# A gated scan and top-1 experts on one core: one page for the expert with most tokens left in place of the last pair of pages, sums of squares of late weights on ScalarE, a load stock of 6500

## The chip, the core and the metric

The kernel runs on one core of one Trainium2 chip. The core has five engines that run side by side and wait for each other by semaphores: TensorE (PE, matmuls; its weight loads are listed apart as PEld), VectorE (DVE), ScalarE (ACT), GpSimd (POOL) and SyncE (SP, which here only issues transfers). Transfers run on 16 DMA engines. The metric is the device time of one execution in microseconds (us), lower is better. Times of different runs are compared by their medians.

## The reference, cut to what matters

```python
# 1. a gated scan along 5056 steps, batch 4, 256 channels
a_t = exp(8 * sigmoid(r_gate) * log(sigmoid(a_param)))
x_gated = sqrt(max(1 - a_t * a_t, 1e-6)) * sigmoid(i_gate) * x
h[t] = a_t[t] * h[t-1] + x_gated[t]            # float32

# 2. its 20224 rows go through one of 8 experts each
logits = h @ w_gate + modality_bias[modality_id]    # two modalities
e = argmax(logits)                                  # the row's expert
out[row] = softmax(logits)[e] * (relu(h[row] @ w1[e]) @ w2[e])   # 256 -> 1024 -> 256
```

On the inputs of the reference, its own routing gives 10124 rows to expert 7, 10051 to expert 4, 49 to expert 2 and none to the others: the bias of the two modalities decides nearly every row.

## The kernel before, in words

**Chunks.** The 5056 steps are cut into 22 chunks (`STEPS`; most have 256 steps, which are 1024 rows of the batch). Of each chunk three arrays (`a`, `g`, `x`) are loaded by SP (L570), go through ACT and DVE (the scan is L656), are split into a high and a low float16 part (L840, L852), are turned by four transposing transfers (`rt`, L893), get their expert (`route_chunk`), and are written row by row into `rows`, a table in DRAM with a region for each expert, by GpSimd's indirect transfers (L1083).

**Pages.** The experts' layers work on pages, which are runs of rows of one expert. Two experts are *hot*, the two that the bias favours, and their weights (`hw`) are converted once at the start. `choose_pages` picks a pair of pages, one for each hot expert, whenever enough rows are written: first a pair of 128 rows, then pairs of 256. When all chunks are routed, it also picks one page of 128 rows for a cold expert (`choose_cold(True)`, called `other`), whose weights are loaded and converted by `cold_weights`; at last come two pairs that take what is left, one of 256 rows and one of 128 (L1275 to L1280). Rows past the end of an expert's region are filled with null rows. Then `over` counts the rows that no page has. Were there any, `more_pages` would run further cold pages after the main part, in rounds.

**A page.** SP reads the place of the page and issues one transposing transfer into `X` (L1320, three buffers) and a small one into `mt` (L1321). TensorE runs layer 1 in four groups of 12 matmuls into `ph` (L1411), ACT and DVE make the two float16 halves of `H` (L1342, L1344). Layer 2 follows one page later, group by group between the next page's layer 1, into `po` (L1451). ACT scales the result (L1363), and GpSimd writes the rows to their places in the output (L1367).

**Weights of a cold page.** `cold_weights` issues two loads of 1 MB (`cr`). `scale_of` sums the squares of each: 16 matmuls of a block with itself (L396), whose diagonal DVE adds up (L399), then a matmul with ones (L403) that adds the partitions; DVE makes a power of two from it (L377 to L383). `convert` makes a high half (L450, L453) and a low half (L433) of `cw`, which a cold page uses as its weights.

**The order.** Nothing is scheduled by hand line by line. Each job is a generator that asks for an engine, with an assumed duration and a condition; `run` always takes the job that could start first, with ranks between jobs that are near. So the assumed durations and conditions set the order in which each engine's instructions stand, and the order stays fixed on the chip. Where `run` foresees a pause of TensorE, it puts in `fill` matmuls without use (L327). `BACKLOG` is a condition of `load_chunk` (L559): a chunk may be loaded once the pages begun so far hold all rows up to and including that chunk's but 5500. Loads, `rt` transposes, pages and weights all stand in SP's one queue.

Of the kernel before, what the change touches and what calls it, by code (L numbers as in the profile page):

```python
# [9 lines left out]
F32 = mybir.dt.float32  # L10
F16 = mybir.dt.float16
BF16 = mybir.dt.bfloat16
I32 = mybir.dt.int32
AF = mybir.ActivationFunctionType
ALU = mybir.AluOpType
AX = mybir.AxisListType

P = 128
B, S, D, E, FF = 4, 5056, 256, 8, 1024
# [22 lines left out]
WAIT = 3.0  # L42
WINDOW = 0.09
PART = 8
BACKLOG = 5500
LOOK = 384
HI = ["A", "AD", "A", "AD", "A", "D"]
LO = "DDPPDD"
# [69 lines left out]
def kernel(  # L118
# [13 lines left out]
    nc = tc.nc  # L132
# [3 lines left out]
    sm = pool("sm", 2)  # L136
# [3 lines left out]
    pso = pool("pso", BUFS["po"], space=bass.MemoryType.PSUM)  # L140
# [70 lines left out]
    ident = const.tile([P, P], F32, name="ident")  # L211
# [68 lines left out]
    def seen(*names):  # L280
        return allof(*[lambda n=n: mark.get(n, FAR) for n in names])

    def room(tag, k=1):

        def at():
            d = slots[tag]
            old = [n - d.bufs for n in range(d.n, d.n + k) if n >= d.bufs]
            return max((d.back.get(n, FAR) for n in old), default=0.0)
        return at

    def take(tag):
        slots[tag].n += 1
        return slots[tag].n - 1
# [4 lines left out]
    def allof(*fs):  # L298
        def at():
            t = 0.0  # L300
            for f in fs:
                t = max(t, f())
                if t >= FAR:
                    break
            return t
        return at
# [6 lines left out]
    def add(gen, prio, t=0.0, urgent=False):  # L313

        th = Thread(gen, prio, t, urgent)
        if th.req is not None:
            threads.append(th)
# [64 lines left out]
        yield "DVE", 0.07, None  # L382
        nc.vector.tensor_scalar(out=vi, in0=si, scalar1=-1.0, scalar2=254.0 * TWO23, op0=ALU.mult, op1=ALU.add)  # L383

    def scale_of(name, raw, sc, iv, factor):

        ss = sm.tile([P, 1], F32, name=f"ss{name}", tag="ss", bufs=16)
        nb = 2 * FF // P
        yield "PE", 0.078 * nb, room("po")
        tp = take("po")  # L390
        pt = pso.tile([P, 512], F32, name=f"pt{name}", tag="po")

        up = raw.bitcast(BF16).rearrange("p (n two) -> p n two", two=2)
        for j in range(nb):
            blk = up[:, j * P : (j + 1) * P, 1]
            nc.tensor.matmul(pt[:, 0:P], blk, blk, start=(j == 0), stop=(j == nb - 1))  # L396
        yield "DVE", 0.3, None
        jk = sm.tile([P, P], F32, name=f"jk{name}", tag="jk", bufs=1)
        nc.vector.scalar_tensor_tensor(  # L399
            out=jk, in0=pt[:, 0:P], scalar=factor, in1=ident, op0=ALU.mult, op1=ALU.mult, accum_out=ss,  # L400
        )
        yield "PE", 0.1, None
        nc.tensor.matmul(pt[:, 256:257], onesf, ss, start=True, stop=True)  # L403
        yield "DVE", 0.07, None
        yield from scale_bits(pt[:, 256:257], sc, iv)
        give("po", tp)
# [95 lines left out]
    def cold_weights(pg):  # L502

        yield "SP", 0.0, seen(("cw", pg.c - 1)) if pg.after else None, 0.0
        for w in range(2):
            yield "DMA", 2.9, room("wr", 4) if w == 0 else None
            if w == 0:
                es = nc.sync.value_load(pg.sel[0:1, 1:2], min_val=0, max_val=E - 1)
                sel_read(pg)
                t = [take("wr") for _ in range(4)]  # L510
                raw = [pm.tile([P, 2 * FF], F32, name=f"cr{pg.c}_{i}", tag="wr", bufs=BUFS["wr"]) for i in range(2)]
                pg.w = [pm.tile([P, 4 * FF], F16, name=f"cw{pg.c}_{i}", tag="wr", bufs=BUFS["wr"]) for i in range(2)]
            raw_load(raw[w], w, es)
        for w in range(2):
            sc = sm.tile([P, 1], F32, name=f"csc{pg.c}_{w}", tag="sc", bufs=4)
            iv = sm.tile([P, 1], F32, name=f"civ{pg.c}_{w}", tag="iv", bufs=4)
            yield "SP", 0.0, None, 0.0
            yield from scale_of(f"c{pg.c}_{w}", raw[w], sc, iv, FACTOR[w])
            def then(w=w):
                give("wr", t[w])  # L520
                mark["cw", pg.c, w] = plan["end"]

            yield from convert(2 * HOT + w, f"c{pg.c}_{w}", raw[w], pg.w[w], sc, (1, 3), False, then)
            if w == 0:
                iv0 = iv
        yield "DVE", 0.07, seen(("cw", pg.c, 0), ("cw", pg.c, 1)), 0.0
        pg.inv = sm.tile([P, 1], F32, name=f"pinv{pg.c}", tag="pinv", bufs=3)
        nc.vector.tensor_tensor(out=pg.inv, in0=iv0, in1=iv, op=ALU.mult)
        pg.tw = t[2:]
        mark["cw", pg.c] = plan["end"]  # L530
# [627 lines left out]
    def queue_page(pg):  # L1158
        pg.n = len(pages)
        pages.append(pg)  # L1160
        if pg.n == 0:
            add(load_rows(), (1, 2), plan["end"])
# [12 lines left out]
    def choose_two(size, full):  # L1175

        sel, ticket = new_sel()
        b2 = tiles["b2", routed(plan["end"]) - 1 if pages else 0]
        z = size / 256
        if full:  # L1180
            d = sm.tile([1, HOT], F32, name=f"d{len(pages)}", tag="d2")
            nc.vector.tensor_tensor(out=d, in0=b2, in1=u, op=ALU.subtract)
            yield "DVE", 0.08, None, 0.0
            nc.vector.tensor_scalar(out=d, in0=d, scalar1=z, scalar2=float(NULLS), op0=ALU.is_lt, op1=ALU.mult)
            yield "DVE", 0.08, None, 0.0
            nc.vector.scalar_tensor_tensor(out=sel, in0=u, scalar=256.0, in1=d, op0=ALU.mult, op1=ALU.max)
            first = plan["end"]
            yield "DVE", 0.08, None, 0.0
            if z == 1:
                nc.vector.scalar_tensor_tensor(out=u, in0=d, scalar=0.0, in1=u, op0=ALU.is_equal, op1=ALU.add)  # L1190
            else:
                nc.vector.tensor_scalar(out=d, in0=d, scalar1=0.0, scalar2=z, op0=ALU.is_equal, op1=ALU.mult)
                yield "DVE", 0.08, None, 0.0
                nc.vector.tensor_tensor(out=u, in0=u, in1=d, op=ALU.add)
        else:
            nc.vector.tensor_scalar(out=sel, in0=u, scalar1=256.0, scalar2=None, op0=ALU.mult)
            yield "DVE", 0.08, None, 0.0
            nc.vector.scalar_tensor_tensor(out=u, in0=u, scalar=z, in1=b2, op0=ALU.add, op1=ALU.min)
        left = [0] * HOT
        for e in range(HOT):  # L1200
            pg = new_page(size, e, sel, e, not full)
            pg.ticket = ticket, left
            queue_page(pg)
        count["chosen"] += HOT * size
# [44 lines left out]
    def over():  # L1249

        ov = sm.tile([1, 1], I32, name=f"over{count['cold']}", tag="over")
        k = left_over(f"o{count['cold']}")
        nc.vector.tensor_reduce(out=ov, in_=k, axis=AX.X, op=ALU.max)
        return ov

    def choose_pages():
        look = lambda: drained(count["chosen"] - LOOK)()
        other, at = None, FAR
        while True:
            yield "DVE", 0.08, allof(enough, room("sel"), look)  # L1260
            if other is None and routed(plan["end"]) == NC:

                add(null_rows(), (0, 5), plan["end"])
                other, at = (yield from choose_cold(True)), len(pages) + 2 * HOT
                add(cold_weights(other), (1, 3), plan["end"])
                yield "DVE", 0.08, room("sel")
            if len(pages) >= at:
                queue_page(other)
                at = FAR
            have = sum(B * t for _, t in CHUNKS[: routed(plan["end"])])  # L1270
            size = 256 if pages else P
            if have - HOT * behind(have) < count["chosen"] + HOT * size:
                break
            yield from choose_two(size, True)
        for size in (256, P):  # L1275
            yield "DVE", 0.08, allof(room("sel"), look, seen("null"))
            yield from choose_two(size, False)
            if at < FAR:
                queue_page(other)
                at = FAR  # L1280

        t = sm.tile([1, HOT, E], F32, name="thot", tag="thot", bufs=1)
        yield "DVE", 0.08, None, 0.0
        for r in range(HOT):
            nc.vector.tensor_scalar(out=t[:, r], in0=hm[:, r], scalar1=u[:, r : r + 1], scalar2=65536.0, op0=ALU.mult, op1=ALU.mult)
        for r in range(HOT):
            nc.vector.tensor_tensor(out=tk, in0=tk, in1=t[:, r], op=ALU.max)
        tiles["over"] = over()
        count["ended"] = True

# [266 lines left out]
```

## Time and profile before

| what | value |
|---|---|
| median of 3 runs | 951.43 us (950.51 to 953.28) |
| the profiled execution, its own time | 951.53 us |
| its span, first to last instruction | 949.8 us |
| idle time of TensorE in the span | 20.3 us (949.8 less 929.5 busy) |
| bytes moved | 155.88 MB, 164 GB/s over the span |
| transfers into X | 81: 78 of 256 rows, 3 of 128 |

The page of the profile gives busy time by engine, then the span in 40 slices of 23.75 us, where a digit is the busy share in tenths. The chain that ended last has two entries only, both after 943 us, so it doesn't help here; the views by time do. In lists of instructions in order of time, the columns are start, duration, engine, line, operation, what it writes and reads, and how often in a row; in brackets stands the idle time of the engine just before and what ended it. Matmuls overlap in such a list, so that the time of one group is read from its start to the next start.

### The profile page before, as it was taken

What the parts mean: (1) busy time and instruction counts of PE and PEld (TensorE: products, weight loads), DVE (VectorE), ACT (ScalarE), POOL (GpSimd) and SP (SyncE); (2) the same over time, 40 slices, a digit from 0 to 9 for tenths busy, and PEclk for the clock granted to TensorE, in tenths of its full rate; (3) what the DMA queues carried; (4) which work ended last, traced back from release to release, by engine and by line L of the source; (5) the groups of instructions that cost most, each with busy time, mean ns of one, the idle gap of its engine ahead of it and who ended that gap; (6) DMA issues with size and microseconds to landing.
All of it is one profiled execution on the core that took longest, in us unless ns stands there. A gap on an engine that the chain in (4) does not pass through costs nothing. (4 is left out here: it accounts for less than half of the span.)

```text
span 949.8 us, 22819 instructions
## 1 busy us (share of the span) xinstructions
PE 929.5 (98%) x8662; PEld 795.5 (84%) x8662; DVE 629.5 (66%) x1458; ACT 578.9 (61%) x805; POOL 509.1 (54%) x761
## 2 busy tenths in 40 slices
PE   8999999999999999999999999999999999999996
PEld 3568777888888888888888888888888888998986
DVE  7988888878787658847675685777577432352321
ACT  8998788566776746665865756575585333333332
POOL 6765676776566565356355625554545435354222
PEclk9999999999999999999999999999999999999999
DMA  8789997889695869586775959596946633532210
GB/s 309 199 209 226 261 207 211 148 233 209 166 225 137 207 165 216 144 193 182 143 184 140 235 92 259 120 209 138 255 120 113 116 70 95 158 85 73 54 41 19
DMA packets 227434, 155.88 MB, mean 164 GB/s; under 512 B 197681, under 2 KB 200882, under 8 KB 227314
## 3 DMA queue, kind: packets, MB, share of 16 engines
q1 hardware_dynamic: 210994, 110.35, 53.9%
q0 software_dynamic: 16176, 43.98, 14.1%
q8 instruction: 69, 1.13, 0.5%
q14 instruction: 51, 0.42, 0.1%
q10 hardware_dynamic: 144, 0.00, 0.0%
HBM read 68.76 MB, written 44.35 MB: 119 GB/s over the span
## 5 line engine op out<-in xcount | busy, mean ns | idle before, releaser
L1411 PE MATMUL ph<-X,hw 128*128 128x256 f16 (+1 forms) x3840 | 463.7, 271 | 7.7 <-DMA X<-rows 7.7
L1451 PE MATMUL po<-hw,H 128*128 128x256 f16 x3840 | 468.9, 273 | 0.0
L1411 PEld LDWEIGHTS <-hw 128*128 128x128 f16 x3936 | 374.2, 98 | 55.3 <-DMA X<-rows 7.4
L1451 PEld LDWEIGHTS <-H 128*128 128x128 f16 x3864 | 374.9, 98 | 45.2 <-issue 1.6
L1344 DVE SCALAR_TENSOR_TENSOR H<-ph,H 128x512 f16<-128x512 f32 (+1 forms) x332 | 220.1, 669 | 233.3 <-ACT H L1342 229.0
L1342 ACT ACTIVATE H<-ph 128x512 f16<-128x512 f32 (+1 forms) x332 | 190.7, 581 | 251.9 <-PE ph L1411 250.0
L1367 POOL DMA_INDIRECT out_dram<-ot,mt x161 | 180.9, 1124 | 192.3 <-ACT ot L1363 139.0
L1083 POOL DMA_INDIRECT rows<-rt,di x158 | 176.1, 1115 | 162.9 <-PE po L1451 63.5
L1363 ACT ACTIVATE ot<-po,gt 128x256 f32<-128x256 f32 x161 | 75.9, 472 | 85.9 <-PE po L1451 79.1
L656 DVE TENSOR_TENSOR_SCAN g<-a,g 128x512 f32<-128x512 f32 (+2 forms) x77 | 94.6, 1241 | 0.6
L639 DVE SCALAR_TENSOR_TENSOR g<-x,g 128x1024 f32<-128x1024 f32 (+2 forms) x39 | 48.2, 1237 | 28.4 <-ACT x L634 28.4
L852 DVE SCALAR_TENSOR_TENSOR a<-g,scy,a 128x512 f16<-128x512 f32 (+3 forms) x88 | 58.7, 694 | 8.6 <-ACT a L840 8.5
L840 ACT ACTIVATE a<-g,scy 128x512 f16<-128x512 f32 (+3 forms) x88 | 55.6, 670 | 6.4 <-DVE scy L687 6.2
L628 ACT ACTIVATE a<-a,ch 128x1024 f32<-128x1024 f32 (+3 forms) x44 | 49.3, 1147 | 0.0
L613 DVE SCALAR_TENSOR_TENSOR g<-g,x 128x1024 f32<-128x1024 f32 (+2 forms) x39 | 48.3, 1241 | 1.1 <-ACT g L607 1.1
L794 DVE TENSOR_REDUCE top<-x 128x4 f32<-128x2048 f32 (+3 forms) x22 | 45.2, 2055 | 3.0 <-DMA x<-in_x_dram 3.0
L327 PE MATMUL fill<-onesb 128*128 128x512 bf16 x178 | 43.4, 392 | 1.1 <-DVE onesb L148 1.1
L634 ACT ACTIVATE x<-x,quarter 128x2048 f32<-128x2048 f32 (+3 forms) x22 | 40.2, 1828 | 0.3
L622 ACT ACTIVATE a<-a 128x2048 f32<-128x2048 f32 (+3 forms) x22 | 38.2, 1736 | 3.6 <-DMA a<-in_r_gate_dram 2.7
L632 ACT ACTIVATE x<-a 128x2048 f32<-128x2048 f32 (+3 forms) x22 | 38.1, 1731 | 3.0 <-DVE g L613 1.7
L607 ACT ACTIVATE g<-g 128x2048 f32<-128x2048 f32 (+3 forms) x22 | 38.2, 1737 | 0.1
L1355 POOL TENSOR_SCALAR gt<-mt,hiv 128x2 f32<-128x2 f32 (+1 forms) x82 | 34.1, 416 | 2.9 <-DMA mt<-rows 0.2
(213 smaller groups left out, 513.1 us busy)
## 6 DMA issues: line engine op xcount, KB each, us to landing
a<-in_r_gate_dram SPq DMA_DIRECT2D x37, 512.0 KB
g<-in_i_gate_dram SPq DMA_DIRECT2D x37, 512.0 KB
x<-in_x_dram SPq DMA_DIRECT2D x37, 512.0 KB
wr<-in_moe_w_dram SPq DMA_DIRECT2D x4, 1024.0 KB
out_dram<-ot,mt POOLq DMA_INDIRECT x161
rows<-rt,di POOLq DMA_INDIRECT x158
cr<-in_moe_w_dram SPq DMA_DIRECT2D x2, 1024.0 KB
rt<-a SPq DMA_TRANSPOSE x88
```

Of the source, the lines that this page charges most:

```text
L613: nc.vector.scalar_tensor_tensor(out=g, in0=g, scalar=1.0, in1=x, op0=ALU.add, op1=ALU.mult)
L628: nc.scalar.activation(sl, sl, AF.Exp, scale=ch[:, h : h + 1], bias=ch[:, h : h + 1])
L656: nc.vector.tensor_tensor_scan(out=gi, data0=ai, data1=gi, initial=0.0, op0=ALU.mult, op1=ALU.add)
L840: nc.scalar.activation(ys[:, 0, :, g], yg[:, :, g, :].rearrange("p h (k b) -> p h k b", b=Q), AF.Copy, scale=sc[:, g : g + 1])
L852: nc.vector.scalar_tensor_tensor(out=ys[:, 1, :, g], in0=yg[:, :, g, :].rearrange("p h (k b) -> p h k b", b=Q), scalar=sc[:, g : g + 1], i ...
L1083: ins = nc.gpsimd.indirect_dma_start(out=rows[:, :], out_offset=bass.IndirectOffsetOnAxis(ap=idx, axis=0), in_=src, in_offset=None, bounds ...
L1342: nc.scalar.activation(t.H[:, 0, hs, :], ph[:, :, 0:st], AF.Relu)
L1344: nc.vector.scalar_tensor_tensor(out=t.H[:, 1, hs, :], in0=ph[:, :, 0:st], scalar=0.0, in1=t.H[:, 0, hs, :], op0=ALU.max, op1=ALU.subtract,)
L1363: nc.scalar.activation(t.ot[:, a, :], po, AF.Copy, scale=t.gt[:, a : a + 1])
L1367: ins = nc.gpsimd.indirect_dma_start(out=out[:, :], out_offset=bass.IndirectOffsetOnAxis(ap=t.mt[:, a, 0:1], axis=0), in_=t.ot[:, a, :], i ...
L1411: ins = nc.tensor.matmul(ph[:, v, 0:st], lhsT, rhs, start=(m == 0), stop=(m == len(mm) - 1))
L1451: ins = nc.tensor.matmul(po, lhsT, rhs, start=(f == 0 and m == 0), stop=(f == NF - 1 and m == len(mm) - 1))
```

## The change

Three parts, and one assumed duration (0.078 to 0.067 for a matmul of a sum).

1. The last pair of pages of 128 rows (one for each hot expert) is gone. In its place `choose_cold(False)` picks one page of 128 rows for the expert with most rows left, of all eight. The page is a cold one: its weights are loaded and converted by `cold_weights`, after those of `other` (`after = True`), whatever its expert is.
2. Sums of squares of cold weights are made by one ACT instruction for each weight array, a Square with an accumulated sum; its output goes to the not yet used `cw` tile (`spare`). The 16 matmuls and the diagonal on DVE are gone for cold weights; those of the hot ones stay.
3. `BACKLOG` goes from 5500 to 6500, by which a chunk may be loaded about 1000 rows sooner.

```diff
-BACKLOG = 5500
+BACKLOG = 6500
...
-    def scale_of(name, raw, sc, iv, factor):
+    def scale_of(name, raw, sc, iv, factor, spare=None):
         ss = sm.tile([P, 1], F32, name=f"ss{name}", tag="ss", bufs=16)
-        nb = 2 * FF // P
-        yield "PE", 0.078 * nb, room("po")
+        if spare is None:
+            nb = 2 * FF // P
+            yield "PE", 0.067 * nb, room("po")
...
+        else:
+            yield "ACT", 2.2, None
+            nc.scalar.activation(spare, raw, AF.Square, scale=factor ** 0.5, accum_out=ss)
+            yield "PE", 0.1, room("po"), 4.0
+            tp = take("po")
+            pt = pso.tile([P, 512], F32, name=f"pt{name}", tag="po")
         nc.tensor.matmul(pt[:, 256:257], onesf, ss, start=True, stop=True)
...
-            yield from scale_of(f"c{pg.c}_{w}", raw[w], sc, iv, FACTOR[w])
+            yield from scale_of(f"c{pg.c}_{w}", raw[w], sc, iv, FACTOR[w], pg.w[w].bitcast(BF16)[:, 0 : 2 * FF])
...
-        for size in (256, P):
-            yield "DVE", 0.08, allof(room("sel"), look, seen("null"))
-            yield from choose_two(size, False)
-            if at < FAR:
-                queue_page(other)
-                at = FAR
+        yield "DVE", 0.08, allof(room("sel"), look, seen("null"))
+        yield from choose_two(256, False)
+        if at < FAR:
+            queue_page(other)
...
             nc.vector.tensor_tensor(out=tk, in0=tk, in1=t[:, r], op=ALU.max)
+        yield "DVE", 0.08, room("sel"), 0.0
+        last = yield from choose_cold(False)
+        last.after = True
+        queue_page(last)
+        add(cold_weights(last), (1, 3), plan["end"])
+        yield "DVE", 0.08, None, 0.0
         tiles["over"] = over()
```

By the order of the built programs TensorE has 96 matmuls of 128 columns less for `hw` pages in layer 1 and 48 more for `cw`, 48 less in layer 2 for `hw` and 24 more for `cw`, none of the 32 sum matmuls of `cr` and two more of L403. There are 182 fills, before 178; the four are among the first 40 us, and none stands behind the beginning of page 4 in either program. The page `other` now stands tenth from the end, before it stood seventh. Up to page 9 (pages are counted from 0 by their transfers into `X`, after the two first ones, which have none), SP's queue is the same.

SP's queue from page 9 on (`X_3060`), before: the pages 10 and 11 come first, and the loads of the next chunk behind the `rt` transposes.

```order
L1320 DMA_TRANSPOSE X_3060<-rows 128x4x256
...
L1320 DMA_TRANSPOSE X_3225<-rows 128x4x256
...
L893 DMA_TRANSPOSE rt_0_3253<-a_2091 128x8x128 x3
...
L1320 DMA_TRANSPOSE X_3327<-rows 128x4x256
...
L893 DMA_TRANSPOSE rt_0_3253<-a_2091 128x8x128
L570 DMA a_3373<-in_r_gate_dram 128x1024 x2
L570 DMA g_3525<-in_i_gate_dram 128x1024 x2
...
L1320 DMA_TRANSPOSE X_3614<-rows 128x4x256
```

The same stretch now, again from page 9 (`X_3064`) to page 12 (`X_3644`):

```order
L1331 DMA_TRANSPOSE X_3064<-rows 128x4x256
...
L577 DMA a_3180<-in_r_gate_dram 128x1024 x2
...
L1331 DMA_TRANSPOSE X_3232<-rows 128x4x256
...
L900 DMA_TRANSPOSE rt_0_3260<-a_2095 128x8x128 x4
...
L1331 DMA_TRANSPOSE X_3356<-rows 128x4x256
...
L577 DMA g_3395<-in_i_gate_dram 128x1024 x2
L577 DMA x_3551<-in_x_dram 128x1024 x2
...
L1331 DMA_TRANSPOSE X_3644<-rows 128x4x256
```

The loads of chunk 9 moved ahead: `a` stands ahead of page 10, and `g` and `x` both ahead of page 12. From page 9 to page 20 the queue now holds the loads of four chunks (9 to 12), before it held two and two thirds.

SP's queue at the end, now: the last page's weights (`cr_0_14486`, `cr_1_14487`) stand ahead of the last three pages, of which `X_14863` is the new one. Before, no weights stood there, and the last two pages had 128 rows for the hot experts.

```order
L1331 DMA_TRANSPOSE X_14396<-rows 128x4x256
...
L515 TENSOR_LOAD sel_14443
...
L480 DMA cr_0_14486<-in_moe_w_dram 128x2x1024
...
L480 DMA cr_1_14487<-in_moe_w_dram 128x8x256
...
L1331 DMA_TRANSPOSE X_14574<-rows 128x4x256
...
L1331 DMA_TRANSPOSE X_14713<-rows 128x4x256
...
L1331 DMA_TRANSPOSE X_14863<-rows 128x4x128
```

ACT's order around the last page's weights, now: a sum of squares (L406) stands behind the first `H` of the fifth page from the end (`H_14580`, counted with the new page as the last) and of the fourth (`H_14723`).

```order
L1353 ACTIVATE H_14580<-ph_0_14581 128x512
L406 ACTIVATE cw_0_14488,ssc_0_14629<-cr_0_14486 128x2048
L1353 ACTIVATE H_14580<-ph_1_14616 128x512
...
L1353 ACTIVATE H_14580<-ph_3_14679 128x512
L457 ACTIVATE cw_0_14488<-cr_0_14486,csc_0_14551 128x1024
L1374 ACTIVATE ot_14598<-po_1_14664,gt_14613 128x256
L457 ACTIVATE cw_0_14488<-cr_0_14486,csc_0_14551 128x1024
L1353 ACTIVATE H_14723<-ph_0_14724 128x512
L406 ACTIVATE cw_1_14489,ssc_1_14761<-cr_1_14487 128x2048
```

Before, the same work for `other` had no L406 and ran its first conversion in one piece:

```order
L1342 ACTIVATE H_13656<-ph_1_13703 128x512
...
L1342 ACTIVATE H_13656<-ph_2_13757 128x512
L450 ACTIVATE cw_0_13555<-cr_0_13553,csc_0_13652 128x1024 x2
L1342 ACTIVATE H_13656<-ph_3_13798 128x512
L1363 ACTIVATE ot_13687<-po_1_13776,gt_13716 128x256
```

Between the two sums ACT still has the evictions of a page's groups (H and ot), as before. On TensorE the matmul that waits for the first sum (L403, now L410) stands behind the fourth group of 12 matmuls of page `H_14580`, the one that waits for the second behind the fourth group of page `H_14723`. Layer 1 of the new page begins two pages after that one's end.

More of the change, by code (lines that the diff above doesn't have):

```diff
@@ L383, in scale_bits @@
         nc.vector.tensor_scalar(out=vi, in0=si, scalar1=-1.0, scalar2=254.0 * TWO23, op0=ALU.mult, op1=ALU.add)
-    def scale_of(name, raw, sc, iv, factor):
+    def scale_of(name, raw, sc, iv, factor, spare=None):
         ss = sm.tile([P, 1], F32, name=f"ss{name}", tag="ss", bufs=16)
-        nb = 2 * FF // P
-        yield "PE", 0.078 * nb, room("po")
[L390 to L402, printed above, removed]
+        if spare is None:
[3 more added lines that the diff above has]
+            pt = pso.tile([P, 512], F32, name=f"pt{name}", tag="po")
+            up = raw.bitcast(BF16).rearrange("p (n two) -> p n two", two=2)
+            for j in range(nb):
+                blk = up[:, j * P : (j + 1) * P, 1]
+                nc.tensor.matmul(pt[:, 0:P], blk, blk, start=(j == 0), stop=(j == nb - 1))
+            yield "DVE", 0.3, None
+            jk = sm.tile([P, P], F32, name=f"jk{name}", tag="jk", bufs=1)
+            nc.vector.scalar_tensor_tensor(
+                out=jk, in0=pt[:, 0:P], scalar=factor, in1=ident, op0=ALU.mult, op1=ALU.mult, accum_out=ss,
+            )
+            yield "PE", 0.1, None
+        else:
+            yield "ACT", 2.2, None
+            nc.scalar.activation(spare, raw, AF.Square, scale=factor ** 0.5, accum_out=ss)
+            yield "PE", 0.1, room("po"), 4.0
+            tp = take("po")
+            pt = pso.tile([P, 512], F32, name=f"pt{name}", tag="po")
         nc.tensor.matmul(pt[:, 256:257], onesf, ss, start=True, stop=True)
```

## The prediction, made before the changed kernel was run

> **What bounds the kernel now.** I read the page first, for which engine is full.
>
> ```profile
> span 949.8 us, 22819 instructions
> PE 929.5 (98%) x8662; PEld 795.5 (84%) x8662; DVE 629.5 (66%) x1458; ACT 578.9 (61%) x805; POOL 509.1 (54%) x761
> PEclk9999999999999999999999999999999999999999
> ```
>
> TensorE is busy for 98% of the span and no other engine for more than two thirds, at a full clock throughout. Then the windows (busy time and, in brackets, instructions of PE, PEld, DVE, ACT and POOL, then clock and DMA share) and the list of waits, for when TensorE is not busy.
>
> ```profile
> 150.00:200.00 50.00, 49.03 (x470) 42.29 (x468) 42.33 (x100) 35.37 (x49) 38.00 (x45) 1.00 0.81 178
> 200.00:250.00 50.00, 50.00 (x473) 43.87 (x472) 38.04 (x81) 35.12 (x46) 30.94 (x41) 1.00 0.91 216
> 925.00:950.00 25.00, 17.25 (x205) 15.77 (x203) 4.09 (x9) 6.03 (x14) 5.66 (x7) 0.94 0.06 18
> ```
>
> ```profile
> PE ph L1411 <- DMA X<-rows: 7.7, 6, 1.9
> ```
>
> Its waits for pages (7.7 us, six times, the longest 1.9) all lie early; the last of them, quoted below, ends at 172.5 us. From there to its last matmul the engine never pauses, as the window from 200 us shows for one stretch. So behind that point the time is TensorE's work, matmul by matmul, plus a tail, and work that goes from it there comes off the end. The end, in order of time:
>
> ```profile
> 934.17 0.83 PE L1411 MATMUL ph<-X,hw 128*128 128x128 f16 x12
> 934.84 0.82 PE L1451 MATMUL po<-hw,H 128*128 128x256 f16 x6
> 935.50 0.83 PE L1411 MATMUL ph<-X,hw 128*128 128x128 f16 x12
> ...
> 938.15 0.83 PE L1411 MATMUL ph<-X,hw 128*128 128x128 f16 x12
> 938.82 3.44 PE L1451 MATMUL po<-hw,H 128*128 128x256 f16 x30
> ...
> 942.42 0.47 ACT L1363 ACTIVATE ot<-po,gt 128x256 f32<-128x256 f32 x1 [2.22 <-PE po L1451]
> 943.17 0.99 POOL L1367 DMA_INDIRECT out_dram<-ot,mt  x1 [1.68 <-ACT ot L1363]
> ```
>
> The matmuls end at 942.3; scaling, writing and the landing of the last rows take the other 7.5 us of the span. The new end has the same tail.
>
> **The pages.** Before, the two last pages take layer 1 of the first of them beside the last page of 256 rows, then layer 1 of the second beside layer 2 of the first, then layer 2 of the second (24 of the 30 matmuls at 938.82). With one page instead, the middle part goes: four steps of 12 matmuls of 128 columns and 6 of 256. The first began at 934.17, the second at 935.50, the fourth at 938.15, so a step takes 1.33 us and the four **5.3 us, which go**. The weights lie in another tile, which changes no matmul's time (columns here: count, busy time, mean ns of one, idle time before):
>
> ```profile
> L1411 PE MATMUL ph<-X,hw 128*128 128x128 f16 x96 | 6.7, 219 | 0.0
> L1411 PE MATMUL ph<-X,cw 128*128 128x128 f16 x48 | 3.3, 219 | 0.0
> ```
>
> **The sums.** `other`'s two sums on TensorE go too; the rows show the first, and the matmul of L403 that stays.
>
> ```profile
> 829.76 1.08 PE L396 MATMUL ptc<-cr 128*128 128x128 bf16 x16
> 830.68 1.47 PE L1411 MATMUL ph<-X,hw 128*128 128x256 f16 x12
> 831.99 0.28 PE L403 MATMUL ptc<-ssc,onesf 128*128 128x1 f32 x2
> 832.13 1.47 PE L1451 MATMUL po<-hw,H 128*128 128x256 f16 x12
> ```
>
> Each sum took 0.92 us from start to start, so **1.8 us less** for two. L403 took 0.14 us, and the new page adds two: **0.3 us more**.
>
> Is a busy TensorE at its limit? [...] Here the next group begins right where 12 matmuls end (1.31 us from 830.68 to 831.99), so I count them in full.
>
> **The last page's weights.** They are new work on SP, DMA, ACT and DVE. No path to the end goes through it unless it is late, and the trace has the same work for `other`:
>
> ```profile
> 816.73 0.38 SPq L473 DMA_DIRECT2D cr<-in_moe_w_dram  x1
> ...
> 844.35 0.16 DVE L528 TENSOR_TENSOR pinv<-civ,civ 128x1 f32<-128x1 f32 x1
> ```
>
> From the issue of the first load to the last conversion 27.6 us. Now the load can go out once DVE has chosen the page, which stands behind the first `H` of page `H_14402`; I allow all of that page's time, 8 groups of 1.31 = 10.5 us. Five pages lie between that page's beginning and the new page's, 52 us. 10.5 + 27.6 = 38, so 14 us are left. ACT and DVE, which do the work, are idle most of the time there (6.0 and 4.1 of 25 us busy in the last window). In SP's queue the last three pages stand behind these 2 MB; `other`'s loads stood among pages likewise, and TensorE waited for none of them, its last wait being at 172.5.
>
> **Sums on ACT.** No row has a Square with an accumulated sum. The nearest is a Square of as many elements; with it stand an `H` and two conversions:
>
> ```profile
> L632 ACT ACTIVATE x<-a 128x2048 f32<-128x2048 f32 (+3 forms) x22 | 38.1, 1731 | 3.0 <-DVE g L613 1.7
> L1342 ACT ACTIVATE H<-ph 128x512 f16<-128x512 f32 (+1 forms) x332 | 190.7, 581 | 251.9 <-PE ph L1411 250.0
> ...
> 832.69 2.19 ACT L450 ACTIVATE cw<-cr,csc 128x1024 f16<-128x1024 f32 x2
> ```
>
> Below it stands at 1.7 us, above I allow twice that, 3.5 us; I take 1.9, near the row. Behind it on ACT wait evictions, which are due some 9 us after their matmuls, since `ph` has four buffers. But TensorE's own L403 matmul waits for it in order. For the first sum of the last page: the first group of page `H_14580` ends 1.3 us in, its `H` on ACT (0.2 after it, 0.6 long) 0.8 later, the sum at 4.0; the matmul stands behind four groups, at 5.2. For the second sum conversions of 1.1 us each come between on ACT, and the same reckoning leaves 0.3 us. Two like it for `other` leave 2.4 and 0.5. With 1.9 nothing waits much; with 3.5 three of the four wait 0.4 to 1.3 us, about 3 in all. I take **0.4 us more**, bounds 0 and 3.
>
> The four more fills lie in the first 40 us, ahead of the waits for pages, which can take them up: 0, and at most their four durations, 1.6 us.
>
> ```profile
> L327 PE MATMUL fill<-onesb 128*128 128x512 bf16 x178 | 43.4, 392 | 1.1 <-DVE onesb L148 1.1
> ```
>
> **The stock.** It moves loads ahead of pages. These rows show what pages did there:
>
> ```profile
> 68.65 0.82 SPq L570 DMA_DIRECT2D a<-in_r_gate_dram  x2
> ...
> 115.99 1.93 SPq L570 DMA_DIRECT2D g<-in_i_gate_dram  x2
> 118.66 1.25 SPq L1320 DMA_TRANSPOSE X<-rows  x1
> ...
> 125.48 6.72 PE L1411 MATMUL ph<-X,hw 128*128 128x256 f16 x60 [1.68 <-DMA X<-rows]
> ...
> 140.49 0.83 SPq L570 DMA_DIRECT2D a<-in_r_gate_dram  x2
> 143.58 1.29 SPq L1320 DMA_TRANSPOSE X<-rows  x1
> ...
> 148.96 5.41 PE L1411 MATMUL ph<-X,hw 128*128 128x256 f16 x48 [1.60 <-DMA X<-rows]
> ...
> 151.28 1.56 SPq L570 DMA_DIRECT2D x<-in_x_dram  x2
> 167.99 1.26 SPq L1320 DMA_TRANSPOSE X<-rows  x1
> ...
> 172.50 5.40 PE L1411 MATMUL ph<-X,hw 128*128 128x256 f16 x48 [0.97 <-DMA X<-rows]
> ...
> 181.09 1.27 SPq L1320 DMA_TRANSPOSE X<-rows  x1
> ...
> 183.06 4.09 PE L1411 MATMUL ph<-X,hw 128*128 128x256 f16 x36
> ...
> 206.81 1.31 SPq L1320 DMA_TRANSPOSE X<-rows  x1
> ...
> 210.49 1.47 PE L1411 MATMUL ph<-X,hw 128*128 128x256 f16 x12
> ```
>
> A page issued with 1 MB of loads just ahead of it came 6.8 and 5.4 us later, one without (page 8) 4.5, and page 12 (206.81) within 3.7 us, without a wait. Page 10 now has the two `a` loads ahead: it goes out at about 182.4 instead of 181.09 (1.3 for their issue) and lands 5.4 to 6.8 later, at 187.8 to 189.2. Page 9 begins at 183.06 with four groups of layer 1 alone, 5.3 us, so TensorE wants page 10 at about 188.4: 0 to 0.8 us of wait. Page 12 has the loads of `x` ahead now, and its rows are hardly earlier, so it lands at 212.2 to 213.6, 1.7 to 3.1 behind 210.49, less what TensorE has already lost. Later pages have more room: before, X was issued one page further ahead from page 13 on. Bounds: 0, if loads end sooner than in those rows, and 3.4 with all of it; I take **1.6 us more**. Behind page 20 the queue is only a chunk ahead.
>
> **The sum**, from the profiled execution's 951.53 us (the median is 951.43, so nothing is corrected): -5.3 - 1.8 + 0.3 + 0.4 + 1.6 = -4.8, **946.7 us**. With all small terms at their best it is 944.7, with all at their worst 951.5 - 6.8 + 3 + 1.6 + 3.4 = 952.7.
>
> **Rivals.**
> - *Late pages eat the gain* (14%). From page 10 to 20 the DMA engines carry one and a third chunks more, where they were 0.81 to 0.91 busy. If besides pages 10 and 12 three or four more wait 1.3 us each (7.7 over six), the waits add up to 6: 951.1. For it: every early wait from 70 us on is one on X, with DMA no busier than it will be. Against it: the four chunks before went out between 68.65 and 152.8, in 84 us, and the four now have eleven pages' time, 115.
> - *Supply becomes the bound, slower* (6%). It decides where a chunk takes longer to come than its four pages take. Then each of the pages 10 to 20 waits 1.3 us, 14 us in all: 951.5 - 6.4 + 14 = 959. Against it: those four chunks took 21 us each, and a chunk's four pages take 42.
> - *The last page's weights are late* (4%). They would have to lose 14 us; a wait of 5 us there gives 951. By the trace such a wait costs itself; after the longest wait for a page, 1.9 us, the clock stays full. [...]
> - *The page is not enough, and further pages run* (3%). 128 + 38 x 256 + 256 = 10112 rows of each hot expert are covered; the reference's 10124 leave 12, which the new page takes, and `other` takes the 49. A miscount would cost at least a load and conversion in the open, 27.6 us, for each of two pages: above 1000.
> - *No new wait at all* (5%): 944.7, or a little less if early waits shrink.
>
> The forecast keeps 68%. Its own range is 944.9 to 948.6. To hold 8 in 10 the range must reach into the first rival: **944.2 to 951.2**. A measurement tells 0.3% (2.9 us) from no change, so faster means below 948.6. Faster: 68 + 5 = 73%; same: 14 + 4 = 18%; slower: 9%.
>
> **What would show it.** TensorE's busy time falls by 6 to 7 us; no L396 on `cr`; 24 matmuls of layer 2 with `cw` right ahead of the tail; the tail still 7.5 us. L406 takes 1.8 to 2.0 us, and the list of waits shows L410 behind ACT with under 1 us. Waits for X rise from 7.7 to about 9, the new ones between 180 and 215 us. The forecast is wrong if TensorE waits behind 250 us, or if new waits for X add up to over 3.4 us.

## The result and the profile after

The changed kernel takes 945.41 us (median of 5 runs, 942.35 to 947.16), the one before 952.16 beside it (5 runs, 950.51 to 953.28): a ratio of 0.993, with a 95% interval of 0.9906 to 0.9953, or 6.7 us less (4.5 to 9.0). The forecast was 946.7, or 4.8 less; the time lies in its range of 944.2 to 951.2 and below the 948.6 that it called faster. The total came out, but in part by luck: the tail was 1.7 us longer than forecast and the waits and the stock cost some 2 us less, and these errors cancelled.

The page of the changed kernel, in the lines that were read of the one before:

```profile
span 940.6 us, 22645 instructions
PE 922.3 (98%) x8566; PEld 789.3 (84%) x8566; DVE 636.4 (68%) x1476; ACT 585.6 (62%) x810; POOL 502.8 (53%) x759
PEclk9999999999999999999999999999999999999999
```

TensorE is busy for 7.1 us less, the span is 9.2 shorter: this execution is the fastest of its five, so some 2.5 us of the 9.2 belong to this execution and not to the change (the medians are 6.7 apart). The waits of its TensorE:

```profile
PE ph L1422 <- DMA X<-rows: 5.2, 5, 1.9
```

Waits for pages fell, from 7.7 to 5.2 us, where 9 were forecast. None comes behind 175 us, and in no row does the L410 matmul wait for ACT. That the change made this fall is not shown: over all traces these early waits add up to 5.5 to 7.7 us with the old pair and to 5.2 to 7.8 with the new page.

To see where the time went, I cut the span of each trace into three: up to the first matmul of page 13 (pages counted from 0, the first behind the early waits), from there to the last matmul, and the tail. The windows view of the kernel before, then of the changed one (columns as in the prediction):

```profile
0.00:220.97 220.97, 208.18 (x1817) 157.97 (x1818) 187.80 (x490) 176.15 (x229) 152.04 (x287) 1.00 0.88 222
220.97:942.25 721.28, 721.28 (x6847) 637.51 (x6844) 441.75 (x969) 402.26 (x575) 356.11 (x474) 1.00 0.63 148
942.25:949.81 7.56, 0.00 (x1) 0.00 (x0) 0.00 (x0) 0.47 (x1) 0.99 (x1) 0.81 0.04 9
```

```profile
0.00:218.49 218.49, 209.63 (x1839) 158.35 (x1840) 189.90 (x496) 178.65 (x231) 148.49 (x285) 1.00 0.89 232
218.49:931.34 712.85, 712.71 (x6730) 630.97 (x6727) 446.54 (x980) 406.50 (x579) 353.33 (x473) 1.00 0.63 150
931.34:940.63 9.29, 0.00 (x0) 0.00 (x0) 0.00 (x0) 0.47 (x1) 0.97 (x1) 0.75 0.05 13
```

The start is 2.5 us shorter, the middle 8.4 (about 1.6 of them work that only moved ahead of page 13, as an experiment shows below), and **the tail 1.7 longer**, though it was to stay the same. In the middle TensorE is busy all the time in both kernels, but for 0.14 us in the changed one. The tail, in the rows of the line that ends the program, on POOL's sequencer (instruction and count, then shortest, median and longest duration in ns, then first and last start in us), before and after:

```profile
L1496 POOLq EVENT_SEMAPHORE  x6: 17/30/43, 946.2 to 946.7; - x6
L1496 POOLq INC_SWDGE_SEM  x1: 564/564/564, 946.7 to 946.7; - x1
```

```profile
L1507 POOLq EVENT_SEMAPHORE  x6: 17/30/43, 935.3 to 937.6; - x6
L1507 POOLq INC_SWDGE_SEM  x1: 544/544/544, 937.7 to 937.7; - x1
```

POOL's six last waits for semaphores took 0.5 us from the first to the last before, and 2.3 after. Five of the six follow each other within 0.4 us; then POOL stands still from 935.70 to 937.58. The rows of the last page had landed at 934.88 by the trace's landing events, so it is not plain what POOL waited for.

### The profile page after: what moved, and what is told of

The parts are those of the page before. It is cut to its first block, busy times and chain, and to the rows that moved or that the text cites. A ratio compares the mean times of both kernels' runs of the same rounds, so it can differ in the third digit from the quotient of the medians.

```text
span 940.6 us, 22645 instructions
## 1 busy us (share of the span) xinstructions
PE 922.3 (98%) x8566; PEld 789.3 (84%) x8566; DVE 636.4 (68%) x1476; ACT 585.6 (62%) x810; POOL 502.8 (53%) x759
## 3 DMA queue, kind: packets, MB, share of 16 engines
q8 instruction: 69, 1.13, 0.5%
## 4 chain that ended last, share of the span: by engine, by line
PE 66%; issue 12%; DMA 6%; POOL 6%; DVE 5%; ACT 2%; SPq 1%; POOLq 0%; ACTq 0%
PE ph L1422 32%; PE po L1462 30%; POOL out_dram L1378 3%; DMA X<-rows 2%; POOL rows L1090 2%; PE fill L327 2%; DVE g L663 1%; DMA wr<-in_moe_w_dram 1%; DVE H L1355 1%; DMA a<-in_r_gate_dram 1%; POOL gt L1366 1%; PE psl L872 1%; DMA rows<-rt,di 1%; DMA x<-in_x_dram 1%; ACT a L847 0%
## 5 line engine op out<-in xcount | busy, mean ns | idle before, releaser
L1462 PE MATMUL po<-hw,H 128*128 128x256 f16 x3792 | 463.5, 273 | 0.2
L1422 PE MATMUL ph<-X,hw 128*128 128x256 f16 x3744 | 457.0, 273 | 5.3 <-DMA X<-rows 5.2
L1422 PEld LDWEIGHTS <-hw 128*128 128x128 f16 x3840 | 368.6, 98 | 51.4 <-DMA X<-rows 7.0
L1355 DVE SCALAR_TENSOR_TENSOR H<-ph,H 128x512 f16<-128x512 f32 (+1 forms) x328 | 217.9, 670 | 224.6 <-ACT H L1353 221.8
L1378 POOL DMA_INDIRECT out_dram<-ot,mt x160 | 175.2, 1095 | 192.1 <-ACT ot L1374 142.9
L1090 POOL DMA_INDIRECT rows<-rt,di x158 | 173.1, 1095 | 167.7 <-PE ph L1422 68.4
L1366 POOL TENSOR_SCALAR gt<-mt,hiv 128x2 f32<-128x2 f32 (+1 forms) x80 | 36.7, 459 | 2.5
```

Of the source, the lines that this page charges most:

```text
L1090: ins = nc.gpsimd.indirect_dma_start(out=rows[:, :], out_offset=bass.IndirectOffsetOnAxis(ap=idx, axis=0), in_=src, in_offset=None, bounds ...
L1355: nc.vector.scalar_tensor_tensor(out=t.H[:, 1, hs, :], in0=ph[:, :, 0:st], scalar=0.0, in1=t.H[:, 0, hs, :], op0=ALU.max, op1=ALU.subtract,)
L1378: ins = nc.gpsimd.indirect_dma_start(out=out[:, :], out_offset=bass.IndirectOffsetOnAxis(ap=t.mt[:, a, 0:1], axis=0), in_=t.ot[:, a, :], i ...
L1422: ins = nc.tensor.matmul(ph[:, v, 0:st], lhsT, rhs, start=(m == 0), stop=(m == len(mm) - 1))
L1462: ins = nc.tensor.matmul(po, lhsT, rhs, start=(f == 0 and m == 0), stop=(f == NF - 1 and m == len(mm) - 1))
```

## The experiments

All ratios are against the kernel before, run beside on the same chip; its median was 950.6, 954.3, 953.8 and 952.1 us in the four groups of experiments, so the us in the table are the ratio times that median, and times of different groups are compared only as ratios. The pieces are those of the one profiled execution of each kernel. TensorE's work has its effect in the middle piece; the first one differs between traces by up to 8 us.

| kernel | ratio (95%) | us against before | to page 13 | page 13 to last matmul | tail |
|---|---|---|---|---|---|
| before | | | 221.0 | 721.3 | 7.6 |
| changed | 0.9930 (0.9906 to 0.9953) | -6.7 | 218.5 | 712.9 | 9.3 |
| stock alone | 0.9997 (0.9984 to 1.0011) | -0.3 | 222.4 | 719.7 | 7.4 |
| page alone | 0.9998 (0.9986 to 1.0010) | -0.2 | 218.1 | 718.1 | 9.8 |
| page alone, 0.067 | 1.0009 (0.9994 to 1.0024) | +0.9 | 225.8 | 718.2 | 9.4 |
| sums alone | 0.9985 (0.9974 to 0.9997) | -1.4 | 220.7 | 719.5 | 7.7 |
| 0.067 alone | 1.0014 (0.9997 to 1.0031) | +1.3 | 222.9 | 721.3 | 8.1 |
| page and sums | 0.9955 (0.9940 to 0.9970) | -4.3 | 222.8 | 715.7 | 9.6 |
| changed, stock 5500 | 0.9931 (0.9918 to 0.9944) | -6.6 | 219.7 | 714.4 | 9.7 |
| changed, sums twice | 0.9977 (0.9959 to 0.9996) | -2.2 | 222.5 | 716.5 | 9.4 |
| changed, 40 never run | 0.9927 (0.9912 to 0.9942) | -7.0 | 221.5 | 714.4 | 7.5 |
| before, 120 never run | 1.0021 (1.0008 to 1.0033) | +2.0 | 223.1 | 721.4 | 9.4 |
| changed, 128 never run | 0.9937 (0.9923 to 0.9951) | -6.0 | 222.4 | 713.6 | 9.2 |
| 40 never run, L410 later | 0.9940 (0.9923 to 0.9957) | -5.7 | 218.6 | 716.1 | 7.4 |

**The stock alone**, on the kernel before:

```diff
-BACKLOG = 5500
+BACKLOG = 6500
```

> The kernel before with the stock of 6500 alone; nothing else of the change. By the prediction's step the pages 10 and 12 wait for their X: +1.6 us, bounds 0 and +3.4, TensorE's busy time unchanged at 929.5, new waits for X between 180 and 215 us. Theory A (the change gains by TensorE's work alone, and the larger stock does nothing): the waits for X stay at 7.7 within 1 us, and the time within 1 us of before. Theory B (the larger stock is what shortened the early waits of the changed kernel from 7.7 to 5.2 us and brought page 8 forward by 4 us): 2 to 4 us faster than before.

No difference (-1.5 to +1.0 us), and no wait behind 175 us. Its timeline where the waits were forecast, SP's rows with the pages 10 and 12 and TensorE's with their first use:

```profile
181.47 0.82 SPq L570 DMA_DIRECT2D a<-in_r_gate_dram  x2
183.04 1.28 SPq L1320 DMA_TRANSPOSE X<-rows  x1
...
187.75 2.79 PE L1411 MATMUL ph<-X,hw 128*128 128x256 f16 x24
...
203.04 1.52 SPq L570 DMA_DIRECT2D x<-in_x_dram  x2
206.06 1.28 SPq L1320 DMA_TRANSPOSE X<-rows  x1
...
211.00 1.25 PE L1411 MATMUL ph<-X,hw 128*128 128x256 f16 x10
```

The loads stand ahead of both pages, as foreseen. Page 10 starts with the second dozen of the 24 matmuls at 187.75, at 189.1, 6.1 us after its issue, and page 12 at 211.0, 4.9 after, both without a wait. By the trace's landing events their X was there at 187.60 and 210.67, each 4.6 us after the issue with 1 MB of loads just ahead, where the two rows that the forecast took it from had 5.4 and 6.8. The DMA engines were no less busy: their share (which can pass 1 in this view) is 1.13 and 1.19 from issue to first use here, and 1.06 and 1.03 in those two rows. So why X came sooner stays open. For page 12, X also went out 0.75 us sooner than in the kernel before and TensorE wanted it 0.5 us later (211.00 against 210.49). The middle piece is 1.6 us shorter only because that much small work of the gates runs ahead of page 13 now: pages 8 to 13 take 1.4 longer.

**The page alone, and the sums alone.** In the first, `cold_weights` calls `scale_of` without a spare tile, with the stock and the planner's number of the kernel before; the second is the kernel before with the spare tile, and so with the sums on ACT. The line in which the two differ from each other, as edited for the first:

```diff
-yield from scale_of(f"c{pg.c}_{w}", raw[w], sc, iv, FACTOR[w], pg.w[w].bitcast(BF16)[:, 0 : 2 * FF])
+yield from scale_of(f"c{pg.c}_{w}", raw[w], sc, iv, FACTOR[w])
```

> One page for the expert with most tokens left in place of the last pair, with the sums of its weights on TensorE as in the kernel before, stock 5500. Theory A: four middle steps go, -5.3 us; two sums of 0.92 and two matmuls of L403 come, +1.8 + 0.3: -3.2 us in time, TensorE's busy time 929.5 - 3.2 = 926.3. Theory B (stock): the same -3.2, and the rest of the 6.7 us of the changed kernel is the stock's. [...]

> The kernel before with the sums of squares of the one page it has of such weights on ACT, all else as before. Theory A: 32 matmuls less, two sums of 0.92: -1.8 us, TensorE's busy time 927.6, no wait of TensorE's for ACT of more than 0.2 us. Rival (TensorE's L403 matmul, or the evictions queued behind the sum on ACT, wait): the row of waits names ACT with 0.4 to 2 us, and the time is -1.4 to +0.2 us against before.

The sums give what was forecast (-1.4, from -2.5 to -0.3, and 1.8 in the middle piece). The page alone does not: its middle piece is 3.2 us shorter, as reckoned, but its time is that of before (-1.3 to +1.0). Part of what is missing is the tail, 9.8 against 7.6; -3.2 + 2.2 = -1.0 lies within the interval.

**The changed kernel with stock 5500** (`BACKLOG` alone put back):

> The changed kernel with the stock back at 5500. Theory A: as the changed kernel, 6.7 us faster than before (within 1.5), waits for X within 1 us of the changed kernel's 5.2. Theory B (the stock earns the shorter early waits): waits for X back at about 7.7 and the time 2 to 4 us above the changed kernel's, 3 to 5 faster than before. By the prediction's step on the stock it would be 1.6 us faster than the changed kernel, 8 faster than before.

-6.6 (-7.8 to -5.3), as the changed kernel. Theory A holds: the stock earns and costs nothing that can be measured.

Between the page alone (-0.2) and this kernel (-6.6) lie the sums on ACT and the planner's number; 3.7 us of the 6.4 are the sums. So the next experiments took these two apart:

```diff
-            yield "PE", 0.078 * nb, room("po")
+            yield "PE", 0.067 * nb, room("po")
```

> The kernel before with the planner's 0.067 us for a matmul of the sums in place of 0.078, nothing else: four more fills and another early order on DVE. By the prediction 0, at most +1.6 us. Theory D (the early order that this number makes is worth the 2 to 3 us by which the page alone fell short of its -3.2): 2 to 3 us faster than before, shorter early waits. Theory S (the short fall belongs to the sums of the last page on TensorE): within 1 us of before.

> The page with its sums on TensorE, stock 5500, the planner's 0.067: the second run of the page alone, with the early order of the changed kernel. Theory A: -3.2 us against before. Theory D: -3, where the same with 0.078 measured -0.4 (-1.3 to +1.0). Theory S: about -0.4 again, and a wait or delay of 2 to 3 us between the last page's sums and its matmuls.

> The page and both pages' sums on ACT, stock 5500, the planner's number back at 0.078: the changed kernel without its two smaller edits. Theory A (TensorE's work alone): -5.3 - 1.8 + 0.3 = -6.8 us against before, TensorE's busy time 922.7. Theory D: about 2.5 us of that is missing, -4.3. Theory S: -6.5, as the kernel with 0.067 and stock 5500 measured.

Theory D falls by the first two runs: the number alone is not faster (-0.3 to +3.0), and with it the page alone is no faster either. In the third its -4.3 came out, but the pieces put what is missing elsewhere: this trace has a wait of 1.0 us behind ACT and a tail 2.0 us longer. Theory S falls too: no wait stands between the last page's sums and its matmuls in the second run's trace. The middle pieces are 0.0, -3.1 and -5.6 against before; the last holds the wait of 1.0 us, quoted below, and would be -6.6 without it. The times of the first two kernels lie about 1 to 2 us above what middle and tail give, that of the changed kernel with stock 5500 1.9 below (-6.9 + 2.2 = -4.7). So of the 2.3 us between page and sums (-4.3) and the same with 0.067 (-6.6), the wait is 1.0 and the rest has no cause that the runs show. These rests are smaller than what the start of a trace varies by, and no single edit goes with them.

**The sums twice.** A second Square ahead of the first:

```diff
+            nc.scalar.activation(spare, raw, AF.Square, scale=factor ** 0.5)
             nc.scalar.activation(spare, raw, AF.Square, scale=factor ** 0.5, accum_out=ss)
```

> The changed kernel with every Square of a weight array done twice on ACT, so that a sum takes 4.0 us there in place of 2.1. By the prediction's reckoning of the wait (3 us for a sum of 3.5): about 3 us slower than the changed kernel. From the changed kernel's trace, where the sums end 2.6, 1.1, 1.3 and 0.9 us ahead of their L410 matmul: 1.9 more leaves waits of 0, 0.8, 0.6 and 1.0, so L410 waits 2.4 us for ACT and the time is 2.4 above the changed kernel's, 4.3 below before. Rival (TensorE has work ahead in its queue that takes such a wait up): no more than 0.5 us slower than the changed kernel.

The waits behind ACT's sums, in the list of this kernel, of the page with sums on ACT, and of the one with 40 instructions never run:

```profile
PE ptc L411 <- ACT cw L407: 2.3, 3, 0.9
```

```profile
PE ptc L410 <- ACT cw L406: 1.0, 1, 1.0
```

```profile
PE ptc L410 <- ACT cw L406: 1.0, 1, 1.0
```

Doubled, three of four matmuls wait 0.8, 0.6 and 0.9 us, as worked out from the gaps; the middle is 3.6 us longer than the changed kernel's, of which some 2.5 are more idle time and the rest counts as busy, and the time is -2.2 (-3.9 to -0.4) against before, 2 us less gained than the -4.3 expected. The 2.3 us of waits stand in these 2.5 in full, so nothing took them up here, and the rival falls. With one Square the traces have 0, 0, 0.3, 1.0 and 1.0 us of it, since ACT gets to the second sum at another time in each: 0.5 on average.

**The tail.** Each of the six traces with the new page so far had a tail of 9.3 to 9.8 us, and a gap of 1.9 to 2.3 us among POOL's last waits; the four with the old pair had none, and 7.4 to 8.1 us. In the built programs POOL has 2,896 instructions with the new page, or 2,898; the gap stood 10 from the end in the first and 12 in the others, so ahead of the same instruction, the 2,887th, in all. With the old pair POOL has 2,902 or 2,904, so there that place comes ahead of the first of these waits. To move it, memsets (instructions of POOL that fill a tile) were put into the branch of further pages, which isn't taken:

```diff
             first, count["ended"] = len(pages), False
+            if left == (N + E * (P - 1)) // P:
+                idle = sm.tile([P, 1], F32, name="idle", tag="idle", bufs=1)
+                for _ in range(40):
+                    nc.gpsimd.memset(idle, 0.0)
```

> The changed kernel with 40 memsets on POOL put into the branch of further pages, which is never taken: nothing more is executed, but the code behind that branch lies 40 instructions further on. In every trace with the new page POOL stands still for 1.9 to 2.3 us among the last semaphore waits, after all rows have landed, always at the same place of its code (10 instructions from the end in the changed kernel, 12 in those that have two more instructions there), and in no trace of the kernels with the old pair. Theory F (the wait is a fetch of the next block of POOL's code, whose border the shorter program of the change has moved among these waits): the gap goes, the tail from TensorE's last matmul to the end of the span is 7.4 to 8.0 us in place of 9.3, and the time is 1.9 us below the changed kernel's, 8.6 below before. Rival L (it belongs to the last page's 12 rows on their way to the output): tail 9.3 and the time as the changed kernel's, 6.7 below before.

> The kernel before with 120 memsets on POOL in the branch that is never taken, so that the end of POOL's code lies against blocks of 128 instructions as it does in the changed kernel. Theory F: a gap of about 1.9 to 2.3 us appears 10 instructions from POOL's end, the tail is 9.3 to 9.8 us in place of 7.5, and the time is 2 us above before. Rival L: no gap, tail 7.5, time as before.

> The changed kernel with 128 such memsets, one whole block: the control for the 40. Theory F: the gap stays at its place, tail 9.3, time as the changed kernel's, 6.7 below before and 1.9 above the one with 40. If any shift of the code took the gap away, the tail would be 7.5 here too. Rival L: tail 9.3 here and with 40.

The same rows of POOL's sequencer, for 40 and 128 on the changed kernel and 120 on the one before:

```profile
L1507 POOLq EVENT_SEMAPHORE  x6: 17/30/43, 939.8 to 940.2; - x6
```

```profile
L1507 POOLq EVENT_SEMAPHORE  x6: 17/30/43, 939.9 to 942.1; - x6
```

```profile
L1496 POOLq EVENT_SEMAPHORE  x6: 17/30/43, 948.6 to 949.0; - x6
L1496 POOLq INC_SWDGE_SEM  x1: 564/564/564, 950.8 to 950.8; - x1
```

With 40 the gap is gone; with 128 it stands where it stood; with 120 the kernel before gets one of 1.7 us, between 949.0 and 950.8 (one instruction later than reckoned), and is 2.0 us slower (0.8 to 3.1). Nothing of what runs differs from the kernel without the memsets. So theory F holds against L: the 1.7 us of the tail belong to the place of POOL's code, not to the last page's rows. It is the traces and the 120 that show it; in the times the kernel with 40 missed what was expected (-7.0, from -8.4 to -5.5, where -8.6 was), and lies 1.0 us below the one with 128, which is within their intervals.

**The L410 matmul later**, on the kernel with 40:

```diff
-            yield "PE", 0.1, room("po"), 4.0
+            yield "PE", 0.1, room("po"), 6.0
```

> The changed kernel with the 40 memsets in the branch never taken, and the planner told to put the L410 matmul of such a sum 6.0 us behind its Square in place of 4.0. With 4.0, L410 waited for the sum in some of the traces (1.0, 0.3, 1.0 us) and in others not. If that wait is the sum's own time on ACT: no wait of L410 for ACT, 713.0 us or less from the first matmul of page 13 to the last one (714.4 with the wait of 1.0), tail 7.5, and the time 7.0 to 7.5 below before. If the later L410 makes the conversions or the last page late instead, TensorE waits ahead of a matmul with cw, and the time is above that of the 40 memsets alone.

The wait is gone, and the middle is 1.7 us longer than with the 40 instructions alone. The group of the fills says why:

```profile
L327 PE MATMUL fill<-onesb x197: 376/379/634, 1.1 to 898.9; 128*128 128x512 bf16 x197
```

There are 15 fills more than in the changed kernel, 10 at 806 and 5 at 898, each 0.22 us from start to start: the planner saw pauses of TensorE behind the later matmul that TensorE doesn't have, and filled them. 3.2 us came for 1.0 saved, and the time missed the 7.0 to 7.5 below before that were expected. Of all versions, the change with the 40 instructions had the lowest ratio, 0.9927, though its interval overlaps those of the change and of its stock at 5500.

## Why the prediction was right, and where not

- **The pages, -5.3, and the sums, -1.8 + 0.3**: right, to 0.2 us in the middle pieces. Page alone 3.2 and 3.1 (forecast 5.3 - 1.8 - 0.3), sums alone 1.8, both 6.9 with 0.067 and 6.6 without, the wait left out (6.8). Each counts in full here, as the prediction took it.
- **"The new end has the same tail"**: wrong, by +1.7 us in the changed kernel and up to +2.2 in others. The mechanism was not among the rivals, and the sum had nothing for it; it is no work of the new page but the change in the length of POOL's code.
- **The stock, +1.6**: mis-sized; measured -0.3 (-1.5 to +1.0). The step that failed is the landing of X behind 1 MB of loads: 5.4 to 6.8 us were taken, 4.6 came at both pages with the stock alone. With 4.6 page 10 has no wait and page 12 has 0.9 by the forecast's own times; this too was absent, since X went out sooner and was wanted later. The bound 0 held; the bound 3.4 is not worked out from the rows, which give 3.1 (0.8 at page 10, and 3.1 less 0.8 at page 12).
- **The sums' wait, +0.4**: 0 in the changed kernel's trace, 0.5 on average over five traces. L406 takes 1.9 us (0.2 more to read the sum), as assumed; doubled, three of the four matmuls wait, 2.3 us in all, where the reckoning with 3.5 had three and about 3.
- **The four more fills, 0 to 1.6**: not settled. The planner's number alone measured +1.3, from -0.3 to +3.0.
- **The last page's weights**: right. Issued at 872.10, ready at 903.9, first used at 920.64: 31.8 us where 27.6 were taken, and 17 left where 14 were.
- **The rivals**: "no new wait at all" describes the changed kernel's waits, but its 944.7 lacked the tail. Late pages, supply, late weights and further pages did not come.

The sum with what was measured: -6.9 of TensorE's work, +1.7 of tail, 0 of stock and 0 to 0.5 of waits is -5.2 to -4.7; the median fell 6.7 (4.5 to 9.0). So the sum lies inside the interval, but near its edge, and some 1.5 to 2 us have no cause that is shown. The same holds with stock 5500 (-4.7 by the pieces, -6.6 measured, from -7.8 to -5.3). If they are real they lie ahead of page 13, in the stretch that took from 218 to 226 us over the traces; what of it this change makes, if any, stays open.

## What to carry to other kernels

Where an engine is never idle over a long stretch, matmul counts times start-to-start durations gave what an edit there is worth to 0.2 us here; measure it on that stretch, since over the traces the start varied by 7.7 us and the tail by 2.4. A change that adds or drops instructions also shifts code, and here that cost or won 1.7 to 2.3 us at a place where POOL had nothing left but waits: a few instructions in a branch that is never taken (here 40 to 128) told this from a real cost. Before a wait is bought off by telling a planner a later time, look at what the planner puts into the pause it then believes in.

## What the runs showed of the hardware

**A border in POOL's code.** In eight of the fourteen traces POOL stands still for 1.7 to 2.3 us among its last waits, a few instructions behind its jump over the branch that isn't taken. The place repeats with 128 instructions: the last six waits start within 2.3 us in the changed kernel, 2.2 with 128 never run, and 0.4 with 40. The page lists two queues of the kind `instruction`, which bring code; on one of them it counts 52 packets in each of these eight traces and 51 in each of the other six. The changed kernel, then the one before (packets, MB, share):

```profile
q14 instruction: 52, 0.43, 0.2%
q14 instruction: 51, 0.42, 0.1%
```

Its large packets have 8,192 bytes, which is 128 instructions of the 64 bytes that they have in the built program. In each of the eight traces one begins 0.1 to 0.7 us into the gap and another 0.7 to 1.0 us behind its end; in the six others none begins later than 0.1 us behind the last of these waits. That the gap is the fetch of the next such block is the reading that fits all of this; no record names the engine that a packet is for. In all fourteen traces 2.5 to 3.2 us pass between the jump and POOL's next recorded instruction, 2.65 in the changed kernel (932.64 to 935.29); whether that is a fetch or a wait, no run decides.

**Half clock after short waits.** In 10 of the 16 cases in all traces in which TensorE waited 1.97 us or more ahead of a matmul, its clock was at half for 3.41 us, from a point between 0.3 us before and 1.3 us behind the end of the wait; after shorter waits never. The page alone with 0.067, where a wait of 2.9 us ends at 135.13 (windows, then timeline):

```profile
120.00:135.00 15.00, 11.41 (x83) 7.75 (x80) 12.42 (x14) 14.13 (x16) 10.06 (x13) 1.00 1.07 231
135.00:150.00 15.00, 14.87 (x135) 12.29 (x136) 10.89 (x30) 8.07 (x11) 8.98 (x9) 0.89 0.67 185
```

```profile
135.13 2.74 PE L1422 MATMUL ph<-X,hw 128*128 128x256 f16 x12 [2.86 <-DMA X<-rows]
...
139.94 1.47 PE L1422 MATMUL ph<-X,hw 128*128 128x256 f16 x12
```

The same twelve matmuls take 2.74 us in place of 1.47. As an estimate, half of the 3.41 us at half clock, such a wait costs up to 1.7 us beside itself. The trace of this kernel has two of them and the longest start of all, 225.8 us. Waits of 2 to 2.9 us were enough to bring the half clock on.
